# Halving the price of TensorE's float32 products in the plan that orders a fused attention and mixture-of-experts kernel

## The chip, the cores and the metric

The kernel runs on one core of one Trainium2 chip. The metric is device time in microseconds (us), the median of several runs. The engines are named PE (TensorE), DVE (VectorE), ACT (ScalarE), POOL (GpSimd) and SP (the queue that issues most transfers).

## The reference

Attention without a score matrix, then two mixtures of experts, all in float32. The part that matters here is the first, on inputs of 4 batches, 8 heads, 576 positions and 64 numbers a head:

```python
q_s = exp(q - max(q, axis=-1)); q_s = q_s / (sum(q_s, axis=-1) + 1e-09)
k_s = exp(k - max(k, axis=2));  k_s = k_s / (sum(k_s, axis=2) + 1e-09)
kv = einsum('bhsd,bhse->bhde', k_s, v)
x = einsum('bhsd,bhde->bhse', q_s, kv)          # 2304 tokens of 512 numbers
logits = x @ w_gate                             # 8 experts
# every token goes to one expert, in the order of the sorted logits, 288 tokens an expert
# h = relu(x @ w1[e]); out = h @ w2[e]; then a second, dense mixture of 4 experts
```

## The kernel before

The program has three stages. The first computes the attention, the logits and the first search (which 288 tokens the first expert gets). The second runs the eight experts, each with a search for the next one beside it, and the third the dense mixture. In each stage the instructions are first recorded and then ordered by a planner, `Plan`. An engine's name on a recorded call leads to `Lane.__getattr__`, which asks `Plan.price` for a duration and hands the call to `Plan.add` (so every recorded instruction carries line 85 in the profile). `Plan.issue` then plays the stage through on a model of the five engines: whichever engine is free first takes, among the instructions whose inputs the model says are ready, the one with the smallest priority number; a price moves when results become ready and the engine free. In the first stage the priority is the length of the chain behind an instruction, summed from the same prices, plus hand-set offsets (`ATT["off"]`). Only the order comes from the model. On the chip each engine executes its list in that order, and waits where a result is missing.

The first stage in the code's names. K arrives in two pairs of batches. `k_max` takes the maximum over the positions: maxima on DVE (`m`), transposes on PE (into the PSUM tile `pm`), a reduction on DVE (`cmx`, `cm`), a transpose back, then the subtraction from K, on DVE or POOL (`k`, `kx`), and the exponential on ACT (`ke`, `kx`). `kv_half` multiplies these by V (tile `va`, products of 65 columns into `pkv`), normalizes the result into `mov` on DVE, transposes it (`pg`, `kvT`) and multiplies it by the gate weights `wg` (8 columns). `q_half` and `q_rest` prepare q (`qm`, `qe`, on DVE or POOL), and `q_cols` does one column of 128 tokens: four transposes on PE (`pa`), an exponential on ACT (`qT`), four products of 146 columns by `mov` into `pkv`, the guard `rq` on ACT (the sum of q plus a small number), its reciprocal on DVE, the logits (`lp` and `logits` on DVE), and the row `xo`, which either DVE computes from PSUM, or ACT copies (`xr`) and POOL multiplies. There are 18 such columns, two of them of the rest rows with eight products on half the rows each. `pkv` has two buffers, which K times V and the columns share; `pa`, `qT` and `rq` have two each, `pm` and `pg` one.

The last six columns are called A to F here. A, C and E go through the buffer pkv_137, B, D and F through pkv_141. The row is computed on DVE for A and D, on POOL for the others. The search follows: for the first twelve columns of `logits` and then for the last six a maximum (`m`), a code of it (`sg`, `key`, `dig`, `dd`), the place of the maximum (`t`, `ct`, `oh`), and a table of comparisons (`ge`), which PE counts.

The functions that the change touches and that use it:

Of the kernel before, what the change touches and what calls it, by code (L numbers as in the profile page):

```python
# [20 lines left out]
B, H, S, D = 4, 8, 576, 64  # L21
# [67 lines left out]
class Plan:  # L89
# [16 lines left out]
    @staticmethod  # L106
    def price(key, name, out, ins):
        n = 1
        for c in out.shape[1:]:
            n *= c  # L110
        m = n
        for i in ins:
            c = 1
            for d in i.shape[1:]:
                c *= d
            m = max(m, c)
        if "dma" in name:
            return (1000.0 if key == "POOL" else 60.0, 4 * n * out.shape[0])
        if key == "PE":
            if name == "transpose":  # L120
                return 110.0
            d = ins[1].dtype
            if d == F32:
                return 85.0 if n == D + 1 else max(n, 128) * 1.7 if n >= 96 else 213.0
            if d == F32R:
                return n / 2.4 + 3
            return max(27.0, n / 2.4 + 3)
        if key == "DVE":
            if name == "tensor_reduce":
                return 70 + 1.04 * m  # L130
            if name == "tensor_scalar" or name == "tensor_copy":
                rate = 0.52 if str(ins[0].space).endswith("SB") and str(out.space).endswith("SB") else 1.04
                return 68 + rate * n + (60 if len(ins) > 1 else 0)
            rate = 0.52 if out.dtype == BF and name == "tensor_tensor" else 1.04
            return 69 + (60 if name == "scalar_tensor_tensor" and len(ins) > 2 else 0) + rate * n
        if key == "ACT":
            return 55 + 0.835 * n
        if key == "POOL":
            if name == "tensor_tensor":
                return 155 + 2.1 * n  # L140
            return 180 + 1.05 * n
        return 60.0
# [895 lines left out]
```

## Time and profile before

| what | us |
|---|---|
| runs, median (lowest, highest) | 1167.06 (1166.71, 1168.41) |
| the profiled execution | 1164.4 |
| its span | 1162.6 |
| attention, up to the last product of F | about 0 to 89.4 |
| first search | about 90 to 112 |
| experts and dense mixture | from 112 on |

The page gives TensorE a busy share of 94% of the span, and from the fifth of its 40 slices to the last but one nine tenths or more; the first stage is where it waits. A timeline row has the start and the length of a group of instructions in us; "x8" is a count of records, and a float32 product leaves two records, a transpose one.

### The profile page before, as it was taken

How to read it: one execution, taken by the hardware profiler on the slowest of the kernel's cores; microseconds unless marked ns; L12 is line 12 of the kernel's file. 1: busy time of each engine (PE TensorE's matmuls, PEld its weight loads, DVE VectorE, ACT ScalarE, POOL GpSimd, SP SyncE). 2: the span in 40 equal slices, each digit the busy share in tenths (PEclk: the TensorE clock that was granted, in tenths of full speed). 3: DMA queues.
4: the chain of work that ended last, by engine and by line, in shares of the span. 5: the costliest groups of instructions: out<-in, count | busy, mean ns of one | idle time of the engine just before them, and what ended most of it. 6: DMA issues, size and time to landing. Idle time of an engine off the chain costs nothing.

```text
span 1162.6 us, 20093 instructions
## 1 busy us (share of the span) xinstructions
PE 1094.0 (94%) x7708; PEld 984.5 (85%) x7708; DVE 714.0 (61%) x1692; ACT 470.7 (40%) x953; POOL 497.7 (43%) x645
## 2 busy tenths in 40 slices
PE   4783999999999999999999999999999999999996
PEld 2672888899999899898899888889998999888995
DVE  5977667867743665655655569655555555555553
ACT  3550555544565544433333345333333333333321
POOL 5562111221212765555554547854443344444322
PEclk9996799999999999999999999999999999999998
DMA  9922788877788421111111111211111111110001
GB/s 274 243 98 92 183 223 206 217 188 201 197 228 218 127 62 57 53 49 56 55 37 55 55 55 55 92 41 51 37 37 54 39 37 37 55 37 19 1 37 54
DMA packets 81760, 113.64 MB, mean 98 GB/s; under 512 B 11520, under 2 KB 56576, under 8 KB 81664
## 3 DMA queue, kind: packets, MB, share of 16 engines
q1 hardware_dynamic: 74080, 86.09, 24.4%
q0 software_dynamic: 7584, 26.27, 10.4%
q8 instruction: 60, 0.98, 0.4%
q14 instruction: 36, 0.29, 0.1%
HBM read 86.08 MB, written 9.48 MB: 82 GB/s over the span
## 4 chain that ended last, share of the span: by engine, by line
PE 77%; DVE 8%; DMA 6%; issue 4%; POOL 2%; ACT 1%; SPq 0%; DVEq 0%; POOLq 0%; ACTq 0%
PE o L85 32%; PE x L85 16%; PE z L85 8%; PE y L85 6%; PE hp L85 6%; PE q L85 4%; DMA raw<-in_moe_w 2%; DMA w<-raw 2%; DMA xg<-x_rows,idx 2%; PE pkv L85 2%; PE sm L85 1%; PE pm L85 1%; PE tp L85 1%; DVE m L85 1%; POOL w L85 1%
## 5 line engine op out<-in xcount | busy, mean ns | idle before, releaser
L85 PE MATMUL o<-w,h 128*128 128x512 f32 x1728 | 535.2, 394 | 4.6 <-DVE h L85 3.0
L85 PEld LDWEIGHTS o<-w,h 128*128 128x128 f32 x1728 | 311.3, 188 | 48.7 <-DVE h L85 4.7
L85 PE MATMUL x<-yops,w 128*128 128x256 f32 (+1 forms) x1536 | 343.2, 295 | 0.6 <-ACT yops L85 0.6
L85 POOL TENSOR_TENSOR w<-raw,w 128x256 fp32r<-128x256 f32 x224 | 170.5, 786 | 313.7 <-ACT w L85 268.2
L85 DVE SCALAR_TENSOR_TENSOR y<-o,prs,y 128x512 f32<-128x512 f32 x270 | 198.8, 749 | 142.4 <-PE o L85 140.0
L85 PEld LDWEIGHTS x<-yops,w 128*128 128x128 f32 x1536 | 262.8, 189 | 21.5 <-ACT yops L85 0.8
L85 ACT ACTIVATE w<-raw 128x1024 fp32r<-128x1024 f32 (+2 forms) x192 | 166.0, 878 | 177.6 <-PE q L85 67.3
L85 PE MATMUL z<-yops,w 128*128 128x256 f32 (+1 forms) x768 | 178.4, 295 | 0.1
L85 ACT ACTIVATE mid<-x 128x256 f32<-128x256 f32 (+1 forms) x192 | 78.1, 408 | 205.9 <-PE x L85 204.5
L85 DVE SCALAR_TENSOR_TENSOR h<-mid,h 128x256 fp32r<-128x256 f32 (+1 forms) x192 | 117.5, 612 | 64.7 <-ACT h L85 63.2
L85 ACT ACTIVATE h<-mid 128x256 fp32r<-128x256 f32 (+1 forms) x192 | 84.7, 441 | 139.4 <-DVE mid L85 139.2
L85 PEld LDWEIGHTS z<-yops,w 128*128 128x128 f32 x768 | 133.0, 189 | 5.2 <-DVE mid L85 0.3
L85 PE MATMUL y<-h,w 128*128 128x288 f32 x768 | 124.9, 302 | 0.7 <-ACT h L85 0.4
L85 PE MATMUL hp<-xT,w 128*128 128x288 f32 x768 | 124.3, 305 | 0.2 <-DVE xT L85 0.2
L85 POOL TENSOR_TENSOR w<-sums,w 128x256 fp32r<-128x256 f32 x128 | 100.2, 813 | 23.2 <-ACT w L85 23.2
L85 PEld LDWEIGHTS hp<-xT,w 128*128 128x128 f32 x768 | 108.4, 192 | 1.5 <-DVE xT L85 0.4
L85 POOL DMA_DIRECT2D w<-raw x32 | 28.8, 900 | 188.8 <-ACT w L85 85.4
L85 PEld LDWEIGHTS y<-h,w 128*128 128x128 f32 x768 | 106.5, 188 | 2.5 <-DMA w<-raw 0.6
L85 PE MATMUL q<-yops,w 128*128 128x256 f32 (+1 forms) x384 | 102.6, 295 | 0.0
L85 PEld LDWEIGHTS q<-yops,w 128*128 128x128 f32 x384 | 70.8, 188 | 7.4
L85 DVE TENSOR_TENSOR mid<-mid,z 128x256 f32<-128x256 f32 (+1 forms) x128 | 57.6, 450 | 30.1 <-PE z L85 17.6
L85 DVE TENSOR_TENSOR mid<-mid,q 128x256 f32<-128x256 f32 (+1 forms) x64 | 28.9, 452 | 53.1 <-PE q L85 48.5
(199 smaller groups left out, 996.8 us busy)
## 6 DMA issues: line engine op xcount, KB each, us to landing
raw<-in_moe_w SPq DMA_DIRECT2D x128, 512.0 KB, 3.8
w<-raw POOLq DMA_DIRECT2D x32, 512.0 KB, 5.9
x_rows<-xo SPq DMA_DIRECT2D x16, 258.5 KB, 2.5
v<-in_v SPq DMA_DIRECT2D x4, 1024.0 KB, 9.9
q<-in_q SPq DMA_DIRECT2D x4, 1024.0 KB, 11.4
k<-in_k SPq DMA_DIRECT2D x3, 1024.0 KB, 9.9
k<-in_k SPq DMA_DIRECT2D x2, 512.0 KB, 6.2
x_rows<-xo SPq DMA_DIRECT2D x4, 129.2 KB, 2.8
```

The source lines that it names most:

```text
L85: lambda: getattr(self.engine, name)(*args, **kw), ins, out, kw.get("start", True))
```

## The change

`Plan.price` gives TensorE's products a duration from the number of columns `n`. For plain float32 operands the price per column is halved, from 1.7 to 0.85 ns, the fixed price of K times V (65 columns, `D + 1`) goes from 85 to 50 ns, and the fixed 213 ns for products under 96 columns becomes 128 x 0.85 = 109 ns.

```diff
             d = ins[1].dtype
             if d == F32:
-                return 85.0 if n == D + 1 else max(n, 128) * 1.7 if n >= 96 else 213.0
+                return 50.0 if n == D + 1 else max(n, 128) * 0.85
             if d == F32R:
                 return n / 2.4 + 3
```

A product by `mov` (146 columns) thus goes from 248 to 124 ns. Transposes (110 ns), the bfloat16 products of the search and the float32r products of the experts keep their prices, so the order of the second and third stages stays as it was, and so does SP's list. In the first stage the lists of PE, DVE and ACT move, POOL's in four places.

The first place is the end of the attention, columns B to F on ACT (`rq_154` and `rq_149` are the two buffers of the guard). Before, from B's copy on:

```order
L85 ACTIVATE xr_161<-pkv_141 128x512
L85 ACTIVATE rq_154<-pkv_141 128x8
L85 ACTIVATE qT_153<-pa_152 128x512
L85 ACTIVATE xr_160<-pkv_137 128x512
L85 ACTIVATE rq_149<-pkv_137 128x8
L85 ACTIVATE qT_148<-pa_147 128x512
L85 ACTIVATE xo_156<-px_125 128x5
L85 ACTIVATE rq_154<-pkv_141 128x8
L85 ACTIVATE qT_153<-pa_152 128x512
```

After, from the same copy on:

```order
L85 ACTIVATE xr_161<-pkv_141 128x512
L85 ACTIVATE qT_153<-pa_152 128x512
L85 ACTIVATE xo_159<-px_125 128x5
L85 ACTIVATE rq_149<-pkv_137 128x8
L85 ACTIVATE qT_148<-pa_147 128x512
L85 ACTIVATE rq_154<-pkv_141 128x8
L85 ACTIVATE xr_160<-pkv_137 128x512
L85 ACTIVATE xo_156<-px_125 128x5
L85 ACTIVATE qT_153<-pa_152 128x512
L85 ACTIVATE xo_151<-px_125 128x5
L85 ACTIVATE rq_154<-pkv_141 128x8
```

B's guard (the first `rq_154`) moved behind C's (`rq_149`) and a `qT`, and D's guard (the second `rq_154`) behind the `qT` that follows it in the old order.

The same place on DVE, where the comparisons of the first twelve columns (`dd`, `oh`, `ge`) meet the logits of E (`lp_150`) and F (`lp_155`). Before:

```order
L85 SCALAR_TENSOR_TENSOR dd_172<-asg_90,dig_168 128x12
L85 TENSOR_TENSOR oh_171<-t_0_169,ct_170 128x96
L85 TENSOR_TENSOR ge_174<-dd_172,jcol_0_80 128x768
L85 RECIPROCAL rq_149<-rq_149 128x8
L85 RECIPROCAL rq_154<-rq_154 128x8
L85 TENSOR_TENSOR lp_150<-pkv_137,rq_149 128x64
L85 TENSOR_TENSOR lp_155<-pkv_141,rq_154 128x64
L85 TENSOR_REDUCE logits<-lp_150 128x8
L85 TENSOR_REDUCE logits<-lp_155 128x8
L85 TENSOR_REDUCE m_164<-logits 128x6
```

After:

```order
L85 RECIPROCAL rq_154<-rq_154 128x8
L85 TENSOR_SCALAR dig_168<-key_167 128x12
L85 TENSOR_REDUCE ct_170<-t_0_169 128x12
L85 TENSOR_TENSOR lp_155<-pkv_141,rq_154 128x64
L85 SCALAR_TENSOR_TENSOR dd_172<-asg_90,dig_168 128x12
L85 TENSOR_TENSOR oh_171<-t_0_169,ct_170 128x96
L85 RECIPROCAL rq_149<-rq_149 128x8
L85 TENSOR_REDUCE logits<-lp_155 128x8
L85 TENSOR_TENSOR lp_150<-pkv_137,rq_149 128x64
L85 TENSOR_TENSOR ge_174<-dd_172,jcol_0_80 128x768
L85 TENSOR_REDUCE logits<-lp_150 128x8
L85 TENSOR_REDUCE m_164<-logits 128x6
```

F's reciprocal moved ahead of `dig`, and the last five steps of the comparison now stand behind and between the logits of E and F.

The second place is the middle, on DVE, behind the maximum `cm` of the second half of K's second pair (`qe_145` is the rest column's subtraction, `mov_0_122` and `mov_0_123` belong to the last two batches). Before:

```order
L85 TENSOR_REDUCE qm_1_158<-q_0_117 128x16
L85 RECIPROCAL rq_149<-rq_149 128x8
L85 TENSOR_TENSOR qe_157<-q_0_115,qm_0_146 128x8x2x64
L85 TENSOR_TENSOR lp_150<-pkv_137,rq_149 128x64
L85 COPY mov_0_122<-pg_139 64x2x8 x2
L85 TENSOR_REDUCE logits<-lp_150 128x8
L85 TENSOR_REDUCE qm_1_163<-qx_0_116 128x8
L85 TENSOR_REDUCE qm_0_146<-q_0_115 128x16
L85 RECIPROCAL rq_154<-rq_154 128x8
L85 TENSOR_TENSOR qe_145<-qx_0_116,qm_1_163 128x512
```

After:

```order
L85 TENSOR_TENSOR cm_134<-cm_134,cmx_144 128x2
L85 TENSOR_TENSOR lp_150<-pkv_137,rq_149 128x64
L85 TENSOR_REDUCE qm_1_158<-q_0_117 128x16
L85 TENSOR_REDUCE logits<-lp_150 128x8
L85 TENSOR_REDUCE qm_1_163<-qx_0_116 128x8
L85 COPY mov_0_122<-pg_139 64x2x8 x2
L85 TENSOR_TENSOR qe_145<-qx_0_116,qm_1_163 128x512
L85 TENSOR_REDUCE qm_0_146<-q_0_115 128x16
```

The large `qe_157` went ahead of `cm`, and `qe_145` stands one maximum (`qm_0_146`) earlier.

A little later on PE, around the products of the second half of K's last batch (`ke_0_136`, `kx_0_110`) and the eight products of the rest column (64x146), as one piece of the difference:

```order
-L85 MATMUL pkv_141<-va_0_119,ke_0_136 64x65 x8
-L85 MATMUL pkv_141<-va_0_119,kx_0_110 64x65 x2
-L85 MATMUL pkv_141<-va_0_119,ke_0_136 64x65 x8
-L85 MATMUL pkv_141<-va_0_119,kx_0_110 64x65 x2
+L85 MATMUL pkv_141<-va_0_119,ke_0_136 64x65 x2
 L85 MATMUL pg_139<-wg,kvT_140 128x8 x2
+L85 MATMUL pa_147<-ident,qe_157 128x128
 L85 MATMUL pkv_137<-mov_0_120,qT_148 64x146
```

Twenty products of K times V stood ahead of the rest column; two of them still do, and the other 18 follow it.

## Rows read from the trace of the kernel before

**Rows 1.** Busy time by stretch: PE, PEld, DVE, ACT, POOL, clock, DMA.

```profile
75.00:89.50 14.50, 13.67 (x112) 12.63 (x112) 11.91 (x42) 8.61 (x30) 7.52 (x6) 1.00 0.44 141
89.50:112.00 22.50, 6.52 (x137) 5.55 (x136) 16.27 (x92) 0.92 (x4) 2.04 (x2) 0.61 0.21 73
```

**Rows 2.** Groups by shape on PE, 0 to 122 us: busy us, mean ns.

```profile
L85 PE MATMUL pkv<-mov,qT 128*128 128x146 f32 x128 | 20.6, 297 | 2.4 <-ACT xo L85 0.7 <-DVE lp L85 0.7 <-DVE mov L85 0.7
```

**Rows 3.** Timeline of PE, products of the last columns: start, length, idle before.

```profile
74.83 2.23 PE L85 MATMUL pkv<-mov,qT 128*128 128x146 f32 x16
...
80.58 1.18 PE L85 MATMUL pkv<-mov,qT 128*128 128x146 f32 x8
...
84.86 1.16 PE L85 MATMUL pkv<-mov,qT 128*128 128x146 f32 x8
85.85 0.60 PE L85 MATMUL pa<-ident,qe 128*128 128x128 f32 x4
86.29 1.16 PE L85 MATMUL pkv<-mov,qT 128*128 128x146 f32 x8
88.18 1.23 PE L85 MATMUL pkv<-mov,qT 128*128 128x146 f32 x8 [0.73 <-ACT xo L85]
```

**Rows 4.** Timeline of ACT, guards of B, D and F, one exponential.

```profile
83.90 0.17 ACT L85 ACTIVATE rq<-pkv 128x8 f32<-128x8 f32 x1
83.95 0.60 ACT L85 ACTIVATE qT<-pa 128x512 f32<-128x512 f32 x1
...
86.10 0.18 ACT L85 ACTIVATE rq<-pkv 128x8 f32<-128x8 f32 x1
...
89.45 0.18 ACT L85 ACTIVATE rq<-pkv 128x8 f32<-128x8 f32 x1 [1.04 <-PE pkv L85]
```

**Rows 5.** Timeline of DVE, from B's reciprocal to the start of the search.

```profile
84.10 0.20 DVE L85 RECIPROCAL rq<-rq 128x8 f32<-128x8 f32 x1 [0.42 <-ACT rq L85]
84.41 0.23 DVE L85 TENSOR_TENSOR lp<-pkv,rq 128x64 f32<-128x64 f32 x1
...
87.35 0.68 DVE L85 TENSOR_TENSOR xo<-pkv,rq 128x512 f32<-128x512 f32 x1
...
88.60 0.17 DVE L85 TENSOR_SCALAR dig<-key 128x12 uint32<-128x12 uint32 x1
...
89.64 0.26 DVE L85 RECIPROCAL rq<-rq 128x8 f32<-128x8 f32 x2
...
90.75 0.20 DVE L85 TENSOR_REDUCE m<-logits 128x6 f32<-128x48 f32 x1
90.99 1.00 DVE L85 TENSOR_SCALAR sg<-m 128x6 int32<-128x6 int32 x1
```

**Rows 6.** Timeline of POOL, two subtractions of K and the last two rows.

```profile
58.38 2.34 POOL L85 TENSOR_TENSOR k<-k,mb 128x1024 f32<-128x1024 f32 x1
...
64.36 2.37 POOL L85 TENSOR_TENSOR k<-k,mb 128x1024 f32<-128x1024 f32 x1
...
89.92 2.04 POOL L85 TENSOR_TENSOR xo<-xr,rq 128x512 f32<-128x512 f32 x2 [1.72 <-DVE rq L85]
```

**Rows 7.** Timeline of DVE in the middle.

```profile
58.53 2.20 DVE L85 TENSOR_TENSOR cm<-cm,cmx 128x2 f32<-128x2 f32 x1
...
61.27 1.22 DVE L85 TENSOR_REDUCE qm<-q 128x16 f32<-128x1024 f32 x1
...
62.52 1.17 DVE L85 TENSOR_TENSOR qe<-q,qm 128x1024 f32<-128x1024 f32 x1
...
64.43 0.68 DVE L85 TENSOR_REDUCE qm<-qx 128x8 f32<-128x512 f32 x1
...
66.26 1.02 DVE L85 TENSOR_TENSOR qe<-qx,qm 128x512 f32<-128x512 f32 x1
...
71.80 0.59 DVE L85 TENSOR_TENSOR mov<-pkv,rs 64x128 f32<-64x128 f32 x2
```

**Rows 8.** Timeline of PE, products of the rest column and those behind it.

```profile
71.75 2.17 PE L85 MATMUL pkv<-mov,qT 128*64 128x146 f32 x20
```

## The prediction

> **What bounds the kernel now.** Only the first of the kernel's three planned stages has plain float32 products, so only its order can move. I read the table of time by stretch first [rows 1]. From 75 to 89.5 us TensorE is busy 13.67 of 14.5 us: there it is the bound. From 89.5 to 112 us it is busy 6.52 of 22.5 us: there a chain between VectorE and TensorE runs alone (the first search), and nothing later can start before it. So what counts is when that chain starts. I take as its start the end of the instruction `sg` on the last six columns of logits, which is 90.99 + 1.00 = 91.99 us [rows 5]. Everything behind it has the order it had, so I let a shift of this point pass in full to the end.
>
> Next I read TensorE's rows for the last six columns, which I call A to F. Their products start at 80.58 (A), 84.86 (D), 86.29 (E) and 88.18 us (F) [rows 3]. TensorE is free of gaps up to F; ahead of F stands 0.73 us of waiting. A column is written into one of two PSUM buffers (A, C, E into one, B, D, F into the other), so D waits until B's buffer has been read, and F until D's has. The readers are the guard `rq` and the copy `xr` on ScalarE, and `lp` or `xo` on VectorE behind the reciprocal of `rq`.
>
> **The new prices against the trace.** A product of 146 columns is two records. Sixteen records take 2.23 us, each about 0.30 us long and overlapping the next [rows 2, 3], so one starts every (2.23 - 0.30) / 15 = 0.13 us and a product lasts 0.26 us. The old price is 146 x 1.7 = 248 ns, the new one 146 x 0.85 = 124 ns. For the 80 products of this kind the planner now believes in less than half of the real time, so it thinks that a column's readers can run sooner and in another order than they can. No instruction gets faster or slower by that: removed and added work are both nothing, and only waits can change.
>
> **Part 1, ScalarE between A and F.** Before, each column's guard came right behind its own products: D's products end at 85.85 and its guard starts at 86.10 [rows 3, 4]. In the new order B's guard stands behind C's guard and a `qT`, and D's guard behind the `qT` that F will read. What is queued behind them is the reciprocal and `lp` on VectorE, and then TensorE itself.
>
> From A's start, with 1.05 us for a column (D takes 85.85 - 84.86 = 0.99, A 1.18 with its tail) and 0.11 us for a transpose (four between 85.85 and 86.29), the old and new orders go as follows.
> Before: A 0, D 4.28, E 5.71, F 7.60 [rows 3].
> After: A 0, B 1.05, seven transposes, C from 2.85 to 3.90, four transposes to 4.35. C's guard starts at 4.15 (0.25 behind its products), `qT` at 4.2 and B's guard 0.5 behind that at 4.7. The reciprocal comes 0.20 later, `lp` 0.31 behind it and 0.23 long [rows 4, 5], and TensorE another 0.15 later (`xo` ends at 88.03, F starts at 88.18): D starts at 5.6, after 1.25 us of idling. D ends at 6.65, E at 7.7. D's guard has to wait for a `qT` that cannot start before D is through, since D's products read the buffer it writes: 6.9 + 0.5 = 7.4. Reciprocal 7.6, `xo` 7.9 for 0.68, `lp` up to 8.75, so F starts at 8.9. That is 1.3 us later than before; hidden by nothing, since TensorE has nothing else left.
>
> **Part 2, VectorE behind F.** Before, from the reciprocals of E and F at 89.64 to the maximum `m` at 90.75 it took 1.11 us. The compare steps of the first twelve columns, from `dig` at 88.60 up to 89.64, took 1.04 us [rows 5] and lay in the shadow of F's products. In the new order F's reciprocal stands ahead of `dig`, so these steps wait for F and then lie on the path. F's products end at 9.95, its guard (1.27 behind F's start [rows 3, 4]) comes at 10.15, its reciprocal at 10.35, and `m` at 10.35 + 1.11 + 1.04 = 12.5, against 90.75 - 80.58 = 10.17. That is 2.3 us.
>
> **Part 3, GpSimd's hold.** The last two `xo` on GpSimd run from 89.92 to 91.96, and `sg`, in line from 90.99, ends only at 91.99; `m` ahead of it, on more numbers, took 0.20, so about 0.8 us of `sg` is waiting [rows 5, 6]. In the new order E's `xo` starts behind E's reciprocal, just ahead of `ge`. If neither `ge` nor `sg` is held, the 2.3 us shrink by these 0.8 to 1.5; if `sg` is held as now, they stay 2.3; if `ge` is held too, `sg` ends up to 0.3 later, 2.6 us. The row of a two-input operation held by GpSimd, `cm` with 2.20 us for 128x2 [rows 7], is nearest to the last case. I take 2.4.
> No row here shows `ge` itself meeting a GpSimd operation. The Trainium skill, SBUF — State Buffer, Who interferes with whom, says that a VectorE instruction with two SBUF inputs and a GpSimd instruction that reads SBUF exclude each other for the whole of whichever came first; by it `ge` is held, and the sum would be 2.6 us; without such a hold it would be 1.5.
>
> **Part 4, the middle (28 to 80 us).** Here products of the first batches go ahead of the transposes of the K maxima, and then the subtractions of K start later, but the two orders meet again: both wait for the same `cm` that GpSimd's subtraction holds from 58.53 to 60.73 [rows 6, 7]. From there I have followed the new order by the rows' durations to A's start and come out 0.1 us from the old 80.58, with six more transposes already done (0.65 us) and about as much more idling. I book it at nothing. What covers it is that TensorE has other columns to do; the price when the cover fails is the first rival. From below, TensorE without any idling would bring A some 2.5 us earlier; from above stands the first rival's 3.0 us.
>
> **Sum.** 0 + 2.4 = 2.4 us. On the profiled execution, 1164.4 us (span 1162.6), that gives 1166.8; the median of the runs shown, 1167.06, lies 2.7 above it, and on that median I predict 1169.5 us. A measurement of this kernel can tell about 0.2%, 2.3 us, from no change, so this lies on the very edge.
>
> **Rival 1, VectorE is held in the middle as well (slower, 1172.4).** In the new order the subtraction `qe` of the rest column stands one maximum earlier. From the end of `cm` VectorE does `lp`, a maximum of 1.22, one of 0.68 and the copies of `mov`, about 2.6 us, then `qe`. GpSimd meanwhile goes from the end of one K subtraction (60.72) to the start of the next (64.36) in 3.64, less the 1.17 for which VectorE's `qe` kept it waiting: about 2.5 us [rows 6, 7]. So the two come to the port nearly together. If GpSimd is first, `qe` waits 2.3 us instead of the 0.4 us that the old one (1.02 for an operation of half of 1.17) waited. Then the rest column starts where it did, at 71.75, but 18 products of the second K half, which used to run ahead of it, now run behind it, and `mov` for the last batch comes at 75.3 instead of 71.80 [rows 7, 8]: 3.5 us, of which TensorE's other work hides 0.5. A is 3.0 us late; with the 2.4 of the end the time is 1167.06 + 5.4 = 1172.4. For it: the near tie. Against it: a quarter of a microsecond decides.
>
> **Rival 2, the middle gives back what the end takes (not slower, 1167.1).** VectorE's `qe` is first at the port, K's second half is finished 2 us sooner, TensorE's idling of the middle (some 3 us from 61 us on, by the same working) shrinks by 2.4 us and A starts at 78.2. It decides the sign from 2.4 us on. For it: six transposes are already done. Against it: A waits for a reader on VectorE then, not for TensorE.
>
> **Rival 3, faster (1164.5).** The same, and the end costs nothing, since the readers of B and D come early enough because TensorE is further ahead. It needs ScalarE to keep up though its order is what delays it.
>
> That the change moves nothing is ruled out: the order shows 185 lines of difference on TensorE alone.
>
> **How the numbers follow.** Forecast 0.38 (half of it above the edge, half below), rival 1 0.36, rival 2 0.19, rival 3 0.07. Slower by over 0.2%: 0.19 + 0.36 = 0.55. Within: 0.19 + 0.19 = 0.38. Faster: 0.07. The range reaches from 1166.4 (a part of rival 2, which leaves out about 0.13 below) to 1173.0 (rival 1 with the 2.6 us of part 3; some 0.07 above).
>
> **What would show it.** In the changed kernel's rows: D's products start over 1 us behind the transposes ahead of them, and so do F's behind E's; the guard of B starts behind C's products, D's behind the `qT`; `ge` of the first twelve columns runs after F instead of during it; from A's start to the end of `sg` it is 13.8 us instead of 11.4. Part 4 is right if A starts within half a microsecond of 80.6; rival 1 if `qe` on 128x512 near 63 us lasts 2 to 3 us and A starts at 83 to 84; rival 2 if A starts before 79. The prediction is wrong altogether if the clock or the stage behind 112 us changes by more than the shift of the search.

## Result and profile after

| | before | after |
|---|---|---|
| runs beside each other, median (lowest, highest), us | 1168.38 (1166.71, 1170.70), 6 runs | 1177.01 (1174.78, 1178.81), 6 runs |
| profiled execution, span, us | 1164.4, 1162.6 | 1176.8, 1175.0 |
| mean granted clock of TensorE | 0.982 | 0.972 |
| A starts, us | 80.58 | 88.84 |
| `sg` on six columns ends, us | 91.99 | 102.57 |

The kernel is slower: ratio 1.0078, interval 1.0061 to 1.0095, 8.6 us between the medians. The prediction was 1169.5 us with a range up to 1173.0; the sign was right, the size was wrong by more than the range allowed. The two spans differ by 12.4 us, and 10.6 of these are there when `sg` ends (102.57 - 91.99); the other 1.8 come behind it. That the medians differ by less has a plain reason: the profiled execution of before lay 4.0 us under its median (1168.38 - 1164.4), that of after lay on it.

The end first, since it is what the forecast was made of. TensorE's products of the last columns in the kernel after (timeline: start, length, engine, line, operation, shape, count, idle time before and its releaser); A and B are the first row, D and E the third, F the last [rows 3]:

```profile
88.84 2.15 PE L85 MATMUL pkv<-mov,qT 128*128 128x146 f32 x16
91.60 1.16 PE L85 MATMUL pkv<-mov,qT 128*128 128x146 f32 x8
94.35 2.23 PE L85 MATMUL pkv<-mov,qT 128*128 128x146 f32 x16 [1.16 <-ACT xo L85]
97.73 1.23 PE L85 MATMUL pkv<-mov,qT 128*128 128x146 f32 x8 [1.16 <-DVE lp L85]
```

Then `ge` in the kernel before, and VectorE and GpSimd behind F in the kernel after [rows 5, 6]:

```profile
89.18 0.55 DVE L85 TENSOR_TENSOR ge<-dd,jcol 128x768 bf16<-128x768 bf16 x1
```

```profile
99.21 0.20 DVE L85 RECIPROCAL rq<-rq 128x8 f32<-128x8 f32 x1 [0.38 <-ACT rq L85]
...
100.29 1.35 DVE L85 TENSOR_TENSOR ge<-dd,jcol 128x768 bf16<-128x768 bf16 x1
...
101.85 0.20 DVE L85 TENSOR_REDUCE m<-logits 128x6 f32<-128x48 f32 x1
102.09 0.48 DVE L85 TENSOR_SCALAR sg<-m 128x6 int32<-128x6 int32 x1
```

```profile
100.19 2.35 POOL L85 TENSOR_TENSOR xo<-xr,rq 128x512 f32<-128x512 f32 x2 [3.76 <-DVE rq L85]
```

D and F each wait 1.16 us where before only F waited, 0.73. `ge` stands behind F's reciprocal and lasts 1.35 us instead of 0.55, since GpSimd's `xo` began 0.10 us ahead of it. In both kernels `sg` ends with GpSimd's last two `xo` (91.99 and 91.96 before, 102.57 and 102.54 after). From A's start to the end of `sg` it is 102.57 - 88.84 = 13.73 us, against 11.41 before: the 2.3 us of the forecast, step by step.

But A itself starts 8.3 us late, where the forecast had booked nothing. The rows of the middle in the kernel after, TensorE first:

```profile
51.03 0.43 PE L85 MATMUL pm<-ident,cm 128*128 128x128 f32 x2 [1.93 <-DVE cm L85]
...
70.33 0.77 PE L85 MATMUL pkv<-mov,qT 128*128 128x146 f32 x4 [2.13 <-DVE lp L85]
71.75 0.74 PE L85 MATMUL pkv<-mov,qT 128*128 128x146 f32 x4 [0.65 <-DVE mov L85]
...
74.90 2.21 PE L85 MATMUL pkv<-mov,qT 128*64 128x146 f32 x16 [0.20 <-DVE lp L85]
...
77.88 0.92 PE L85 MATMUL pkv<-va,ke 128*64 128x65 f32 x12
```

VectorE's subtraction `qe` of the rest column, GpSimd's subtraction of K beside it, and the multiplication into `mov` of the last batch [rows 7]:

```profile
66.02 2.76 DVE L85 TENSOR_TENSOR qe<-qx,qm 128x512 f32<-128x512 f32 x1
...
80.37 0.59 DVE L85 TENSOR_TENSOR mov<-pkv,rs 64x128 f32<-64x128 f32 x2
```

```profile
65.88 2.35 POOL L85 TENSOR_TENSOR k<-k,mb 128x1024 f32<-128x1024 f32 x1
```

This is rival 1 as it was written: GpSimd's subtraction starts 0.14 us ahead of `qe` (so it is first at what the prediction calls the port, which lets one of the two through at a time), `qe` lasts 2.76 us, the K products run behind the rest column (77.88 against 74.90), and `mov` comes at 80.37 instead of 71.80. It does not make 8.3 us, though; the 16 records of the rest column take 2.21 us, and 1.22 us at full clock (after_filled, below). The same stretches by engine (columns: stretch, length, busy us of PE, PEld, DVE, ACT, POOL, then the granted clock, DMA share and GB/s), kernel after:

```profile
52.20:59.00 6.80, 6.45 (x86) 5.21 (x84) 4.75 (x10) 2.06 (x4) 0.64 (x3) 0.50 0.72 185
72.60:79.40 6.80, 6.51 (x57) 5.14 (x58) 1.74 (x8) 2.79 (x8) 2.97 (x3) 0.50 0.22 80
75.00:89.50 14.50, 12.81 (x120) 10.66 (x121) 8.43 (x26) 5.24 (x18) 5.47 (x5) 0.85 0.29 96
89.50:112.00 22.50, 11.37 (x131) 10.11 (x129) 13.75 (x67) 5.86 (x21) 5.48 (x5) 0.73 0.27 93
```

and the first two of them in the kernel before:

```profile
52.20:59.00 6.80, 6.01 (x89) 4.77 (x88) 5.89 (x19) 4.03 (x10) 2.63 (x4) 1.00 0.91 248
72.60:79.40 6.80, 6.68 (x60) 5.85 (x61) 4.99 (x17) 3.84 (x13) 4.72 (x3) 1.00 0.48 171
```

In the kernel after the granted clock falls twice to 0.50, the lower of its two levels (1.2 GHz), from 52.2 to 59.0 and from 72.6 to 79.4 us; in the profiled execution of before it stays at 1.00 there. Ahead of the falls TensorE had waited 1.93 us (up to 51.03), and 2.13 and 0.65 us (up to 71.75). So two causes were on the table: the order, and the clock.

### The profile page after: what moved, and what is told of

Its sections match the earlier page's. It is cut to its first block, busy times and chain, and to the rows that moved or that the text cites. A ratio compares the mean times of both kernels' runs of the same rounds, so it can differ in the third digit from the quotient of the medians.

```text
span 1175.0 us, 20085 instructions
## 1 busy us (share of the span) xinstructions
PE 1102.3 (94%) x7708; PEld 990.9 (84%) x7708; DVE 714.3 (61%) x1692; ACT 470.5 (40%) x953; POOL 497.3 (42%) x645
## 3 DMA queue, kind: packets, MB, share of 16 engines
HBM read 86.08 MB, written 9.48 MB: 81 GB/s over the span
## 4 chain that ended last, share of the span: by engine, by line
PE 77%; DMA 7%; DVE 5%; issue 4%; SPq 2%; POOL 2%; ACT 1%; POOLq 0%; DVEq 0%; ACTq 0%
PE o L85 31%; PE x L85 16%; PE z L85 8%; PE y L85 6%; PE hp L85 6%; PE q L85 4%; SPq L85 2%; DMA w<-raw 2%; DMA raw<-in_moe_w 2%; PE pkv L85 2%; DMA xg<-x_rows,idx 2%; PE sm L85 1%; PE tp L85 1%; POOL w L85 1%; DVE yops L85 1%
```

## The experiments

All of them rest on one idea. The kernel records the same instructions under either price, so both orders can be worked out in it, and each engine's list put together from pieces of both. Three pieces are used: up to about 67 us, from there to A, and from A on, cut where before and after have had the same instructions on every engine. The core of it, the same in all but one of the kernels (`b` is the order of before, `a` that of after; numbers in `move` and `fill` are the recorded instructions' own; of the `pl.MIX` lines below the entries `cuts` and `base` are left out, and ranges are written short):

```diff
+        return order
+
+    def issue(self, tc):
+        order = self.plan_order()
+        if self.MIX:
+            order = self.mix(order)
         with tc.manual_schedule():
             for i in order:
-                self.ops[i][2]()
-        return max(free.values())
...
+            cuts = [0] + [c[key] for c in self.MIX["cuts"]] + [None]
+            rows = {w: [i for i in o if mine[i][0] == key] for w, o in lists.items()}
+            seq[key] = [i for w, x, y in zip(self.MIX["take"], cuts, cuts[1:]) for i in rows[w][x:y]]
```

The times at which the clock fell and rose are read from stretches of 0.2 us; each row below gives those ahead of 92 us. All ratios are against runs of before on the same chip.

### Which piece of the order

```diff
+pl.MIX = {'take': 'bba'}   # tail_only
+pl.MIX = {'take': 'aab'}   # all_but_tail
+pl.MIX = {'take': 'abb'}   # first_part_only
+pl.MIX = {'take': 'bab'}   # middle_only
```

**tail_only.** 

> The lists of the kernel before up to the last column but six, from there on (column A and the search) those of the kernel after. Prediction's parts 1 to 3: A starts at 80.6 us as before, from A's start to the end of sg on six columns 13.7 us instead of 11.4, the time 2.3 us (0.2%) over the kernel before, ratio 1.002. Rival: the end of after costs 2.3 us only because the middle had put its engines out of step; then A to sg is 11.4 to 12.5 us here and the ratio is 1.000 to 1.001.

**all_but_tail.** 

> The lists of the kernel after up to column A, those of before from A on. If the middle and the end add up: A starts at 88.8 us as in the kernel after, A to sg 11.4 us, the time 2.3 us below the kernel after, 6 to 8 us over the kernel before, ratio 1.005 to 1.007. If the end's 2.3 us hang on the middle, A to sg stays at 13 us or more and the time is that of the kernel after, ratio 1.008.

**first_part_only.** 

> The lists of after only for the first part (up to about 67 us: 254 of TensorE's rows), before's from there on. Theory clock: the granted clock falls to 0.5 near 52 us as in after, since the gap ahead of the transpose of cm at 51.0 us is in this part; the second half of K starts 2.6 us later (transposes of cm at 63.4 instead of 60.8), and A is 2.6 to 3.5 us late, ratio 1.002 to 1.003. Theory cover (prediction's part 4): TensorE's other work hides it, A at 80.6 to 81.1, ratio 1.000.

**middle_only.** 

> The lists of after only for the middle (the 90 rows of TensorE from about 68 us to A), before's on both sides. Theory clock: the granted clock falls to 0.5 behind 70 us and A is 5 us or more late, ratio 1.004 or more. Theory order (rival 1 of the prediction): the clock stays at 1.00 and A is 3.0 to 3.5 us late, since the 18 products of K by V run behind the rest column, ratio 1.003. Theory that it needs the late first part: A within 1 us of 80.6, ratio 1.000 to 1.001.

| kernel | ratio, interval | A starts | A to end of `sg` | clock at 0.50 |
|---|---|---|---|---|
| tail_only | 1.0056, 1.0033 to 1.0079 | 85.41 | 13.83 | 53.2 to 56.6 |
| all_but_tail | 1.0038, 1.0021 to 1.0055 | 87.51 | 11.88 | 40.6 to 44.0, 71.4 to 78.2 |
| first_part_only | 1.0015, 0.9994 to 1.0036 | 80.64 | 11.94 | never |
| middle_only | 1.0054, 1.0030 to 1.0079 | 85.38 | 11.83 | 63.0 to 66.4 |

Three things follow. First, the end costs what parts 1 to 3 said, with either middle ahead of it: 13.8 us from A to `sg` with the lists of after, 11.8 to 11.9 with those of before (11.4 in before itself), so 1.9 to 2.4 us. Second, the first piece by itself is hidden: `cm` ends at 60.76 + 1.11 = 61.87 us, 1.1 late, and A starts at 80.64, so there the cover of part 4 holds, and the fall of the clock that was expected near 52 us did not come. Third, the middle by itself makes A late: between `mov` of the third batch and that of the last lie 77.97 - 70.88 = 7.09 us in middle_only, against 71.80 - 68.27 = 3.53 before. VectorE in middle_only:

```profile
67.31 1.33 DVE L88 TENSOR_TENSOR qe<-qx,qm 128x512 f32<-128x512 f32 x1
70.88 0.59 DVE L88 TENSOR_TENSOR mov<-pkv,rs 64x128 f32<-64x128 f32 x2
...
77.97 0.59 DVE L88 TENSOR_TENSOR mov<-pkv,rs 64x128 f32<-64x128 f32 x2
```

`qe` is hardly held here (1.33 us), and the 7.09 us are there all the same: the place of the K products makes them, not the hold. (Whether A waits for this `mov` is another question; see the last experiments.) The ratio of all_but_tail, 1.0038, lies under the 1.005 to 1.007 expected.

tail_only missed its number, for two reasons that its rows show. Its `mov` of the last batch came at 74.50 instead of 71.80, 2.7 us late, although its lists up to there are those of before. TensorE in tail_only:

```profile
53.10 1.02 PE L88 MATMUL pkv<-va,ke 128*64 128x65 f32 x14 [2.08 <-ACT ke L88]
```

These K products do not wait in the kernel before. What differs is not the lists but how the engines' lists are interleaved when they are written: before_filled (below), with the same lists in before's own interleaving, runs these products at 50.97 without a wait. That the wait was thereby tied to a later `ke` is inferred, not shown. The granted clock then fell from 53.2 to 56.6 us. middle_only, which also begins with before's piece, has the same wait of 2.08 us, and its `cm` ends at 62.33 instead of 60.73. So the ratios of these two are too high by what that wait cost, by estimate some 2 us; the differences inside their middles and ends hold.

Another 2.1 us (85.41 - 80.58 - 2.70) come just ahead of A, on GpSimd in tail_only:

```profile
80.28 1.90 POOL L88 TENSOR_TENSOR qe<-q,qm 128x1024 f32<-128x1024 f32 x1 [1.09 <-PE pa L88]
82.14 1.04 POOL L88 TENSOR_TENSOR xo<-xr,rq 128x512 f32<-128x512 f32 x1
```

The new order puts the rest column's `xo` behind the last `qe`, which waits for TensorE; before it stood ahead. ScalarE's next guard waits 1.71 us for this `xo`; behind the guard is queued the `qT` for which TensorE's transposes ahead of A wait 1.03 us, and A itself waits another 0.49 for an `xo` on VectorE. It is one of the four swaps on GpSimd that the prediction did not cost, read from the rows and not tried by itself.

### Fillers for the clock, first attempt

Transposes of the identity into unused columns of a PSUM tile were put on TensorE ahead of its long waits.

```diff
+pl.MIX = {'take': 'aaa', 'fill': [(374, 12), (603, 14), (584, 4)]}   # after_fill_both
+pl.MIX = {'take': 'aaa', 'fill': [(374, 12)]}   # after_fill_first
+pl.MIX = {'take': 'aaa', 'fill': [(603, 14), (584, 4)]}   # after_fill_second
...
+                nc.tensor.transpose(pg[:, 256:384], ident, ident)
```

**after_fill_both.** 

> The order of after; 12 transposes of the identity into unused columns of pg stand on TensorE ahead of the transposes of cm that wait 1.93 us at 49.1 us, 14 and 4 ahead of the products that wait 2.13 us at 68.2 and 0.65 us at 71.1 us. They add no result. Theory clock: the granted clock stays at 1.00 up to A; what ran at half speed (52.3 to 59, 72.5 to 79 us) takes half as long, A starts at 84 to 85 instead of 88.8 us, ratio to before 1.003 to 1.005. Theory order: the clock follows the waits and costs nothing of its own; A stays at 88 to 89 us, ratio 1.008. If the fillers stand in the way: later than 89.

**after_fill_first.** 

> The order of after with the first 12 fillers alone (gap at 49.1 us). Theory clock: the first fall (52 to 59 us) is gone, the second stays; the transposes of the second cm start at 62.9 to 63.4 instead of 63.39 us, since most of the first fall lies beside VectorE's and GpSimd's work; A 0.5 to 1 us earlier than in after. If the second fall hangs on the first: it goes too and A starts at 84 to 85 us.

**after_fill_second.** 

> The order of after with the fillers at 68.2 and 71.1 us alone. Theory clock: the first fall stays, the second (72.5 to 79 us) is gone, and A starts 3 to 4 us earlier, at 85 to 86 us, ratio to before 1.004 to 1.006. Theory order: A at 88 to 89 us, ratio 1.008.

| kernel | ratio, interval | A starts | clock at 0.50 |
|---|---|---|---|
| after_fill_both | 1.0094, 1.0057 to 1.0130 | 93.04 | 41.2 to 48.0, 58.2 to 61.6, 72.0 to 78.8 |
| after_fill_first | 1.0079, 1.0052 to 1.0106 | 88.33 | 40.4 to 43.8, 71.0 to 78.0 |
| after_fill_second | 1.0103, 1.0049 to 1.0157 | 86.92 | 63.2 to 66.6 |

These did not decide it: the falls went to places with no fillers, and in after_fill_both the second set waited itself, because its tile was still being read:

```profile
72.96 3.25 PE L751 MATMUL pg<-ident 128*128 128x128 f32 x14 [2.39 <-DVE mov L88]
```

What they did show is that the same instructions have their falls at other times in each execution: up to 49 us the three and the kernel after have the same lists, and the clock fell at 41.2 and 40.4 us in the first two, and not before 52 us in after_fill_second and after. after_fill_second, with only one short fall, still had A at 86.92, 6.3 us late: by this row most of the lateness was not the clock.

### One link at a time in the middle

```diff
+pl.MIX = {'take': 'aaa', 'move': [(list(range(548, 566)), 542)]}   # after_kv_ahead
+pl.MIX = {'take': 'aaa', 'move': [([591, 588], 541)]}   # after_guard_back
+pl.MIX = {'take': 'aaa', 'move': [([591, 588], 541), ([476], 511), (list(range(548, 566)), 542)]}   # after_chain_back
+pl.MIX = {'take': 'aaa', 'move': [([671], 412)]}   # after_qe_early
```

**after_kv_ahead.** 

> The order of after, with one move on TensorE: the 18 products of K by V (second half of the last batch) that stood behind the rest column stand ahead of it again, as before. Theory order: mov of the last batch comes at about 76 instead of 80.4 us, A 3 us or more earlier (85 to 86), ratio 1.005. Theory clock: they run at half speed ahead of the rest column as well as behind it, the rest column waits for them, and A is 0 to 2 us earlier, ratio 1.006 to 1.008.

Ratio 1.0125, 1.0097 to 1.0153: slower still, and the expectation of either theory missed. The clock was at 0.50 from 52.4 to 59.4 and from 72.8 to 86.6 us, longer than in after, so how much of this the move itself cost stays open. Moved ahead, the K products meet a wait nobody had reckoned with; TensorE, then GpSimd:

```profile
75.97 1.14 PE L88 MATMUL pkv<-va,ke 128*64 128x65 f32 x16 [1.73 <-POOL va L88]
```

```profile
75.31 0.61 POOL L88 COPY va<-v 128x512 f32<-128x512 f32 x1
```

GpSimd's copy of V for the last batch stands behind two `xo` in the new order, and these wait for the guard of a column. So the place of the K products is a late link of a chain over ScalarE and GpSimd.

**after_guard_back.** 

> The order of after with one move on ScalarE: the copy xr and the guard rq of the column whose products start at 70.3 us stand ahead of kvT again, as before. In after they wait for kvT, which waits for TensorE's transposes of mov at 72.3 us; the reciprocal on VectorE idles 2.18 us (to 73.78) for it. Theory chain (guard late, so GpSimd's copy of V behind that column late, so the 18 products of K by V late): the reciprocal comes near 71.2, GpSimd's copy of V ends 2.5 us earlier (73.2 instead of 75.7), the rest column starts 0.5 to 1 us earlier; A gains 1 us at most, since the 18 products still stand behind the rest column on TensorE; ratio 1.007. Theory that this guard is the whole of the middle: A 4 to 5 us earlier at an equal clock, ratio 1.004.

Ratio 1.0106, 1.0072 to 1.0140. The copy of V ended at 74.68 instead of 75.67 us, A started at 88.66 instead of 88.84: as the chain theory said of A, though by less at the copy, and the ratio missed its 1.007. The clock fell as in after (0.50 from 51.8 to 58.8 and from 72.2 to 79.2 us).

**after_chain_back.** 

> The order of after with the whole chain of the middle put back: the guard ahead of kvT on ScalarE, the copy of V for the last batch ahead of two xo on GpSimd, the 18 products of K by V ahead of the rest column on TensorE. Theory chain: what made the 18 products alone cost time (they waited 1.73 us for GpSimd's copy of V) is gone; mov of the last batch comes 3.5 to 4 us behind that of the third batch, as before (68.27, 71.80), instead of 9.4; the start of A is 4 to 5 us earlier at an equal clock, ratio 1.003 to 1.005. Theory that VectorE's hold of qe sets it: A gains 1 us at most, ratio 1.007.

Ratio 1.0078, 1.0051 to 1.0106, with the clock at 0.50 from 51.8 to 58.6 and from 65.4 to 75.6 us. `mov` still came 80.21 - 71.25 = 8.96 us behind that of the third batch, A at 88.68. With so much at the lower clock this said little.

**after_qe_early.** 

> The order of after with one move on VectorE: the subtraction qe on 128x512 stands right behind its maximum, ahead of the two copies of mov, so that it reaches the port shared with GpSimd before GpSimd's subtraction of K does (65.5 against 65.9 us). Rival 1's hold priced alone: qe takes 0.6 to 1.0 us instead of 2.76, the products at 70.3 us start 1.5 to 2 us earlier, and A as much at an equal clock, ratio 1.006. If something else holds those products: no change, ratio 1.008. If GpSimd is first after all: qe lasts 2.4 us or more, ratio 1.008.

Ratio 1.0066, 1.0049 to 1.0084. GpSimd was first after all (its subtraction of K began at 64.18 us, `qe` at 64.33), and `qe` lasted 2.75 us. The move missed the port by 0.15 us, so the hold was not priced here; the clock was at 0.50 from 63.4 to 73.8 us, and A started at 87.28.

### True prices

```diff
-                return 85.0 if n == D + 1 else max(n, 128) * 1.7 if n >= 96 else 213.0
+                return 60.0 if n == D + 1 else n * 1.78 if n >= 96 else 180.0
```

**price_measured.** 

> The kernel before with prices as the trace measures them: K by V 60 ns, a product of 146 columns 260 ns, one of 8 columns 180 ns. If true prices make a good order: ratio 0.995 to 1.000. If the old order was good because its numbers had been chosen together with the old prices, any other price lands on another order of about the quality of after: ratio 1.002 to 1.010.

Ratio 1.0069, 1.0046 to 1.0091. Prices close to the trace give an order about as slow as the halved ones do, as the second expectation said. So it is not nearness to the trace that makes the old order the faster one. That the hand-set offsets of the priority had come to fit the old prices would explain it, but no run tried other offsets: that is not shown.

### Fillers that hold the clock

Second attempt, with a tile that is free at each wait, and for the order of before too.

```diff
+pl.MIX = {'take': 'bbb', 'fill': [(242, 6, 'pm'), (374, 11, 'pg'), (469, 14, 'pm'), (638, 4, 'pm'), (603, 3, 'pm'), (584, 4, 'pm')]}   # before_filled
+pl.MIX = {'take': 'aaa', 'fill': [(242, 6, 'pm'), (374, 12, 'pg'), (469, 9, 'pm'), (603, 14, 'pm'), (584, 4, 'pm')]}   # after_filled
+pl.MIX = {'take': 'aab', 'fill': [(242, 6, 'pm'), (374, 12, 'pg'), (469, 9, 'pm'), (603, 14, 'pm'), (584, 4, 'pm')]}   # after_filled_old_end
```

**before_filled.** 

> The order of before, with transposes of the identity into unused columns (42 in all, of no use to the result) on TensorE ahead of six waits of the attention: 6 at 39.2, 11 at 48.9, 14 at 60.8, 4 at 63.8, 3 at 67.6 and 4 at 69.0 us. Theory: before's own spread (1163 to 1173 us) is falls of the granted clock in the attention, at other places in each execution, which such idling brings on. Then no execution falls ahead of 90 us, the mean clock is 0.981 to 0.983 and the time 1164 to 1165.5 us, 2 us under the median of before, ratio 0.997 to 0.9985. Rival: the falls do not follow TensorE's idling; then the spread stays and the ratio is 1.000 or, if the fillers stand in the way, 1.001 to 1.003.

**after_filled.** 

> The order of after with such fillers: 6 at 38.7, 12 at 51.0, 9 at 63.4, 14 at 70.3 and 4 at 71.8 us. If they keep the clock at 1.00 up to A, what is left over before_filled is the order's own price at full clock. Theory order: 5 to 7 us (the end 2.3, the middle 3 to 5), time 1170 to 1172, ratio to before 1.003 to 1.005. Theory clock: 2.3 to 3 us, ratio 1.000 to 1.001. If falls remain: 1.006 or more, and the split stays open.

**after_filled_old_end.** 

> after_filled with the lists of before from column A on. At full clock the difference to after_filled is the price of the end: prediction's parts 1 to 3 say 2.3 us, ratio 0.002 under that of after_filled. If seam effects rule (the end alone cost before's order 5 us, though A to sg took only 2.4 more): 0 to 5.

In the profiled executions of all three no fall is left up to 92 us. Before_filled, then after_filled, by stretch:

```profile
18.00:92.00 74.00, 64.64 (x686) 54.28 (x686) 62.15 (x163) 39.66 (x109) 42.96 (x34) 1.00 0.68 182
```

```profile
18.00:92.00 74.00, 62.45 (x660) 51.48 (x661) 58.07 (x141) 36.94 (x99) 39.69 (x31) 1.00 0.65 174
```

That makes their rows comparable at one clock:

| kernel | ratio, interval | last `cm` ends | rest column | A | `sg` ends |
|---|---|---|---|---|---|
| before_filled | 1.0013, 0.9994 to 1.0032 | 60.95 | 71.98 | 80.81 | 92.11 |
| after_filled | 1.0086, 1.0063 to 1.0110 | 62.35 | 73.72 | 85.61 | 99.33 |
| after_filled_old_end | 1.0045, 1.0024 to 1.0065 | 62.41 | 73.78 | 85.39 | 96.63 |
| after_filled_fixed | 1.0055, 1.0036 to 1.0075 | 63.06 | 73.29 | 84.71 | 98.43 |
| after_filled_norm_back | 1.0076, 1.0051 to 1.0100 | 62.65 | 74.67 | 86.08 | 99.81 |

The order alone costs 99.33 - 92.11 = 7.2 us: 2.7 at the end (99.33 - 96.63) and 4.5 ahead of it (96.63 - 92.11). The profiled execution of after ended `sg` at 102.57, 3.2 us later than after_filled; that is taken as the cost of its two falls of the clock.

The late `cm` (62.35 instead of 60.95) is a hold too. In the new order the large `qe` stands ahead of `cm` on VectorE. Its row overlaps the start of GpSimd's subtraction of K, which then lasts 3.33 us (2.37 in before_filled), and `cm` ends with that subtraction. VectorE and GpSimd in after_filled_fixed, the fourth kernel of the table, where `cm` ends at 63.06:

```profile
58.80 2.03 DVE L88 TENSOR_TENSOR qe<-q,qm 128x1024 f32<-128x1024 f32 x1
```

```profile
59.72 3.33 POOL L88 TENSOR_TENSOR k<-k,mb 128x1024 f32<-128x1024 f32 x1
```

Where TensorE's time went between the rest column and A is seen in its rows; in after_filled:

```profile
73.72 1.22 PE L88 MATMUL pkv<-mov,qT 128*64 128x146 f32 x16
...
76.54 2.07 PE L88 MATMUL pkv<-mov,qT 128*128 128x146 f32 x12
...
82.22 0.66 PE L88 MATMUL pa<-ident,qe 128*128 128x128 f32 x4 [0.76 <-ACT qT L88]
...
85.44 0.33 PE L88 MATMUL pa<-ident,qe 128*128 128x128 f32 x1 [0.76 <-ACT qT L88]
85.61 2.15 PE L88 MATMUL pkv<-mov,qT 128*128 128x146 f32 x16
```

and in before_filled:

```profile
71.98 2.17 PE L88 MATMUL pkv<-mov,qT 128*64 128x146 f32 x20
...
80.81 1.18 PE L88 MATMUL pkv<-mov,qT 128*128 128x146 f32 x8
```

From the rest column to A it is 11.89 us instead of 8.83. Of these 3.06 us, 1.20 are the K products that now stand there (75.34 to 76.54), and 1.52 are two waits of 0.76 for a `qT` on ScalarE; before_filled has no wait in that stretch.

The runs say less than the rows. The ratio of after_filled is above the 1.006 from which on its expectation left the split open, that of after_filled_old_end lies 0.0041 under it where 0.002 was expected and the rows give 2.7 us, and before_filled was not faster than before (1.0013), and after_filled not faster than after (1.0086 against 1.0078), though both profiled executions lost no clock in the attention. In before_filled the clock fell behind it (0.50 from 160.4 to 167.0 and from 361.8 to 371.8 us), in the experts' stage, whose order neither the change nor the fillers touch. The products of that stage behind a wait, and the stretch that follows:

```profile
359.96 1.29 PE L88 MATMUL y<-h,w 128*128 128x288 f32 x6 [1.87 <-ACT h L88]
```

```profile
360.00:370.20 10.20, 10.20 (x50) 9.11 (x51) 3.40 (x8) 4.93 (x7) 1.73 (x2) 0.59 0.83 221
```

In the profiled execution of before TensorE has no such wait there and its clock stays at 1.00.

So the forecast that the fillers would make before 2 us faster fell, and no kernel here beats before.

### The hold, and the last links

```diff
+'move': [([591, 588], 541), ([476], 511), (list(range(548, 566)), 542), ([671], 412)]   # after_filled_fixed
+'move': [([591, 588], 541), ([476], 511), (list(range(548, 566)), 542), ([566], 630), ([567, 568, 569], 628)]   # after_filled_norm_back
```

The third kernel, after_filled_norm_first, has the moves of the second, `'take': 'baa'` and other counts of fillers (11, 14 and 8 at three of the waits instead of 12, 9 and 14).

**after_filled_fixed.** 

> The order of after with fillers (4 instead of 14 at 70.3 us) and four moves back in the middle: guard ahead of kvT on ScalarE, copy of V ahead of two xo on GpSimd, 18 products of K by V ahead of the rest column on TensorE, and qe ahead of the copies of mov on VectorE. Theory: these are the middle's price at full clock; A starts 3 to 5 us earlier than in after_filled and the ratio is 0.003 to 0.004 under it. If the late first part (cm 1.6 us late) is the middle's price: 1 us or less.

Here `qe` won the port. VectorE and GpSimd in after_filled_fixed:

```profile
65.46 0.69 DVE L88 TENSOR_TENSOR qe<-qx,qm 128x512 f32<-128x512 f32 x1 [0.24 <-PE pa L88]
```

```profile
65.61 2.77 POOL L88 TENSOR_TENSOR k<-k,mb 128x1024 f32<-128x1024 f32 x1
```

From the end of `cm` to A it is 84.71 - 63.06 = 21.65 us, against 85.61 - 62.35 = 23.26 in after_filled and 80.81 - 60.95 = 19.86 in before_filled: 1.6 of 3.4 us came back. A itself started only 0.9 us earlier than in after_filled, less than the 3 to 5 expected, while the ratio came out 0.0031 lower, as expected.

**after_filled_norm_back.** 

> after_filled with the middle's chain undone to its last link: guard rq ahead of kvT on ScalarE, copy of V ahead of two xo on GpSimd, 18 products of K by V ahead of the rest column on TensorE, and, new here, the guard rs of that product ahead of the rest column's copy and guard on ScalarE, with its reciprocal and the two multiplications into mov ahead of that column's on VectorE; qe stays where after has it. In after_filled_fixed, without that link, mov of the last batch still came 7.31 us behind that of the third (7.09 in after_filled, 3.54 in before_filled). Theory chain: now it comes 3.5 to 4.5 us behind, column A starts 2.5 to 3.5 us earlier than the 85.6 of after_filled, and the ratio is 0.002 to 0.003 under that of after_filled (1.0086). If the lateness is made further ahead (the maximum of K): 7 us again, A within 1 us of 85.6.

With the hold as in after (`qe` 2.77 us) and the chain undone to its end, `mov` came 75.03 - 70.34 = 4.69 us behind that of the third batch, little more than the 3.5 to 4.5 expected. A did not move: 86.08 - 62.65 = 23.43 us from `cm`. So A does not wait for `mov` of the last batch (in after_filled, too, TensorE's transposes of it start at 78.45 without a wait). Of the moves tried, the hold of `qe` is what the middle's time hangs on: up to the rest column the lists of this kernel and of after_filled_fixed differ only in the place of `qe` and in ten fillers, which end ahead of a wait of 0.46 us, and the rest column comes 74.67 - 62.65 = 12.02 us behind `cm` with the hold, and 73.29 - 63.06 = 10.23 without. The other links, once undone, were paid again as three waits on ScalarE between the rest column and A. TensorE in after_filled_norm_back:

```profile
77.35 1.73 PE L88 MATMUL pkv<-mov,qT 128*128 128x146 f32 x12 [0.99 <-ACT xo L88]
...
82.69 0.66 PE L88 MATMUL pa<-ident,qe 128*128 128x128 f32 x4 [0.75 <-ACT qT L88]
...
85.92 0.33 PE L88 MATMUL pa<-ident,qe 128*128 128x128 f32 x1 [0.76 <-ACT qT L88]
86.08 2.15 PE L88 MATMUL pkv<-mov,qT 128*128 128x146 f32 x16
```

For the last two the rows of ScalarE show why: each `qT` stands behind the guard, once behind copy and guard, of products that TensorE has only just done. ScalarE in after_filled_norm_back, then in before, where two `qT` run ahead of such a guard:

```profile
81.97 0.18 ACT L88 ACTIVATE rq<-pkv 128x8 f32<-128x8 f32 x1 [1.24 <-PE pkv L88]
82.05 0.59 ACT L88 ACTIVATE qT<-pa 128x512 f32<-128x512 f32 x1
...
84.62 0.60 ACT L88 ACTIVATE xr<-pkv 128x512 f32<-128x512 f32 x1 [0.93 <-PE pkv L88]
...
85.27 0.60 ACT L88 ACTIVATE qT<-pa 128x512 f32<-128x512 f32 x1
```

```profile
77.59 1.21 ACT L85 ACTIVATE qT<-pa 128x512 f32<-128x512 f32 x2 [1.12 <-PE pa L85]
78.70 0.17 ACT L85 ACTIVATE rq<-pkv 128x8 f32<-128x8 f32 x1
```

This is read from the rows; no run put these `qT` ahead of the guards.

**after_filled_norm_first.** 

> The same with the lists of before up to about 67 us, so that the maximum of the last half of K comes as before (its end at 60.7 to 61 instead of 62.35 us). If the two add up, column A starts another 1.3 to 1.6 us earlier, at 80.8 to 81.5 us, and what is left over before_filled is the end alone: from A's start to the end of sg 13.7 us, that end at 94.5 to 95.3 (92.1 in before_filled), ratio 1.002 to 1.004. If the first part's lateness is absorbed, as it was with before's lists behind it: A where after_filled_norm_back has it.

Ratio 1.0108, 1.0082 to 1.0134. It begins with before's piece and so has the wait of 2.08 us for `ke` again; its clock fell behind that (at 0.50 from 53.6 to 56.8 us), and VectorE's reduction ahead of `cm` waited 3.32 us for the fillers, which were written to the tile that it reads:

```profile
63.77 0.42 DVE L88 TENSOR_REDUCE cm<-pm 128x2 f32<-128x256 f32 x1 [3.32 <-PE pm L751]
```

So `cm` ended at 64.92 instead of 61 us, and A came at 88.63, 23.71 us behind. It gave no answer on the first piece: with before's lists the large `qe` (66.71, 1.17 us) stands behind `cm`, so the stretch from `cm` to A is not the same work either.

## Why the prediction missed

**Part 1 (ScalarE's guards), right.** F was to start 8.9 us behind A instead of 7.6, and started 97.73 - 88.84 = 8.89 behind it. D waited 1.16 us, 1.25 was worked out.

**Part 2 (VectorE's compare steps), right.** `ge` ran behind F, and `m` came 13.01 us behind A (101.85 - 88.84) where 12.5 was worked out. `ge` being held makes 0.8 of it (1.35 instead of 0.55 us); the other steps took 0.3 less than worked out.

**Part 3 (GpSimd's hold), right.** 2.4 of 1.5 to 2.6 was taken; 2.3 was measured in after, 2.5 at one clock (13.72 against 11.24 us in after_filled and after_filled_old_end). `ge` was held, 1.35 us instead of 0.55. Here the Trainium skill, SBUF — State Buffer, Who interferes with whom, says that a VectorE instruction with two SBUF inputs contends with a GpSimd instruction that reads SBUF, and that the order of issue decides which of the two is blocked. The rows of `ge` agree, and so do those of `qe`, 2.77 us behind GpSimd (after_filled) and 0.69 ahead of it (after_filled_fixed).

**Part 4 (the middle at nothing), wrong; this is the step that failed.** At one clock A starts 85.61 - 80.81 = 4.8 us late. The late maximum of K makes 1.4 of it (`cm` ends at 62.35 instead of 60.95): both orders do wait for the `cm` that GpSimd's subtraction holds, as the text said, but in the new one that subtraction is itself held by the large `qe` (3.33 us instead of 2.37). With before's lists behind it this lateness was hidden, as the cover said (first_part_only); that the new middle does not hide it is read from the rows, and no run separated it, since the new order has moved 1.2 us of work (that `qe`) from behind `cm` to ahead of it. The remaining 3.4 us are the new middle's: 1.6 to 1.8 for the hold of the rest column's `qe` (after_filled_fixed against after_filled and after_filled_norm_back). The rest, some 1.7, is put down to the waits on ScalarE, which none of the moves took away; that share is read from rows, not shown by a run. I had followed TensorE and VectorE through the middle, and of ScalarE and GpSimd only what stood next to them; the swaps on those two (guard behind `kvT`, the copy of V behind two `xo`, `xo` behind `qe`) were never costed.

**Rival 1, at 0.36 against 0.38, had the hold right and its consequence wrong.** The hold took place as described. That its price of 3.0 us is near the 3.4 that the middle added at one clock is luck: the late `mov`, from which the 3.0 came, is not what A waits for.

**What no case contained: the clock.** The text said that a change of the clock by more than the shift would make it wrong altogether, and gave that no chance. The two falls in the attention go with 3.2 us in the profiled execution of after, against after_filled. That before's profiled execution had none there was the better end of what it does, not its habit: it lay 2.7 us under the median that the forecast was made on, which I noted and did not ask about. Of the 89 runs of before beside these experiments, the nine at a mean clock of 0.974 took 1170.9 us on average, the nine at 0.982 or 0.983 took 1164.4. By that slope, 0.76 us for 0.001, the mean clock of the six runs of after (0.9738, against 0.9787 over the runs of before) would be worth 3.7 of the 9.6 us between the means. That is an estimate; after_filled, whose six runs had 0.9785, were no faster than after, so the clock's share in the medians stays open, and with it how far the order brings falls about.

Open too: what the two waits of 0.76 us would give back with `qT` ahead of the guards, what GpSimd's swap of `xo` and `qe` costs alone, and why the medians put the end at more than the rows do (0.0041 of the ratio, 4.8 us, against 2.7).

## What to carry to other kernels

A change to a planner's prices is a change to every queue: cost the swaps on the engines that are not the bound as carefully as those on the one that is, since a copy behind a waiting instruction there is what the bound waits for later. Where hand-set offsets sit beside prices, prices nearer to the trace need not give a better order (1.0069 here). And before the trace of one execution is taken as the kernel, its mean clock and time are to be held against the other runs'; a term for the clock then belongs in the range.

## What the runs showed of the hardware

The granted clock falls at other times in executions that run the same instructions. Up to 60 us the kernels after, after_guard_back, after_qe_early and first_part_only have the same lists; the first fall came at 52.2 and 51.8 us in the first two, at 63.4 in the third, and in the fourth none came in the attention at all; the second and third ran on the same chip. The Trainium skill, TensorE: Matmul & The Clock Gate, Part 1, says that what watches TensorE's activity runs freely and does not start with the kernel; the rows agree with it.

Ahead of these falls TensorE had waited (1.93 us at 51.03 and 2.13 at 70.33 in after, 1.87 at 359.96 in before_filled), but the same or a similar wait passes without one elsewhere: before waits 1.82 us ahead of 60.79 and keeps 1.00. So here a list's waits do not tell whether a fall comes, and one profiled execution is a draw. That two executions of one kernel thus differ by some 6 us (before at a mean clock of 0.974 and of 0.982 or more) was not expected either.

Which of two operations 0.15 us apart gets the port decides over 2 us: `qe` at 64.33 behind GpSimd's 64.18 took 2.75 us, at 65.46 ahead of its 65.61 it took 0.69.
